# Fused memory attention and two-layer MLP on one core: order of the start, halves of the first weights, and the place of every operation from a table

## The chip, the cores and the metric

The kernel runs on one NeuronCore of a Trainium2 chip. The metric is device microseconds of one execution: three runs of the kernel before took 557.5, 558.44 and 559.41 us, median 558.44. The profiled execution has a span (first to last instruction) of 555.3 us. Engines are named as in the profile: PE (TensorE products), PEld (its weight loads), DVE (VectorE), ACT (ScalarE), POOL (GpSimd) and SP, whose queue issues every DMA here.

## The reference

For 4 batches, 8 heads, 576 rows and head size 64, causal softmax attention is mixed by a gate with a linear memory read, and the result, as 2304 rows of 512, goes through a two-layer MLP with a leaky unit. Inputs are 64-bit or 32-bit floats as given; the MLP's weights arrive as 64-bit floats.

```python
scores = scale * np.matmul(q, k.transpose(0, 1, 3, 2))      # causal mask, softmax -> a
local = np.matmul(a, v)
q_p = np.where(q > 0, q, np.exp(q) - 1.0) + 1.0
mem_out = (q_p @ M_prev) / (q_p . z_prev + 1e-6)
x = g * mem_out + (1 - g) * local                           # g = sigmoid(beta), per head
h = x.reshape(2304, 512) @ w_in                             # 512 x 2048
out = (np.maximum(h, 0) + alpha * np.minimum(h, 0)) @ w_out # 2048 x 512
```

## The kernel before, in words

Rows are worked in nine groups of 256. Group Z (called the first group here) holds the first 64 rows of each of the four batches; each batch's other 512 rows make two groups, of row blocks 1 and 2 and of row blocks 3 and 4. The first group is short attention in f32 (64 keys), and so are blocks 1 and 2 of batch 0; all later groups split each f32 operand into two f16 parts and multiply three of the four combinations.

A group's way is this. Scores (PE, tile s) go through mask and row minimum on DVE, exponent with row sum on ACT, and a scaling into two f16 parts P on ACT and DVE (`unit_probs`; the memory read's columns come from POOL). SP transposes P by a DMA into PT. PE multiplies PT with the values into tile bank (`pair_values`, for two heads at a time, a "pair" here), ACT and DVE make the two f16 parts xn, SP transposes them into x. Then `moe_in` gives tile h (PE), ACT and DVE make the leaky unit's r and gg, and `moe_out` gives tile y (PE), which ACT scales to the output. A step j of the MLP is 256 of the 2048 hidden columns; h has two PSUM buffers and y two.

The weights arrive as raw 64-bit words in pieces of two times 512 KB, `load_w`. For each, `conv_w` builds f32 on DVE with three bit operations (`to_f32`, lines 770 to 777) over 1024 columns, and ACT adds up their squares; from the sums come power-of-two scales. The first half of w_in and w_out (pieces 0 to 3 and 4 to 7) is used in f32 by the first group and by batch 0's first group (steps 0 to 3), and all pieces are then split into f16 parts. Where the first group begins, `load_first` fetches its q, z, k, v and M rows, `first_scores` and `first_values` make its attention, and `WARM` gives 16 + 50 products of a constant (tile h from ones) that nothing reads; they keep PE working while the first transfers land.

The order of all this is not the order in the file. `Work.add` records each operation with its dependencies and an estimated price (`price`), and `issue` (line 532) lays out all engines by list scheduling with ranks that a table of biases by phase (`STAGES`) shifts, over three passes (`lay`, line 462). What comes out is one order of all operations; each engine then runs its own in that order, and so does SP's queue with the DMAs. Nearly every operation is issued from line 560, so the profile is read by tiles. Names: q_0_93 (q2_0) holds the first group's q rows, R the big weight buffer in which also the first group's k, v and M rows stand, kn and E staging for weights, k_65 and v_66 the turned keys and the split values.

Of the kernel before, what the change touches and what calls it, by code (L numbers as in the profile page):

```python
# [2 lines left out]

# [21 lines left out]
WARM = 16, 50  # L25
# [6 lines left out]
STAGES = [  # L32
    (2, {
        "A0": 10.6, "A:DVE": 50.6, "BK0": 102.5, "BK:ACT": -27.7, "BK:PE": 3.4, "C0": -56.4, "C1": 22.3, "C2": 335.8,
        "C3": -920, "C:ACT": 1096.2, "C:DVE": -3.8, "C:PE": -943.6, "I": -699.2, "I:DVE": 79.2, "I:POOL": 497.7,
        "J:ACT": 470.6, "J:DVE": 108, "J:PE": -179.3, "K": 47.5, "K:POOL": 2.3, "L0K": -713.8, "L0K:DMA": 228.2,
# [6 lines left out]
        "LW:DMA": 605.3, "LZ": 27.3, "LZ:DMA": -1145.9, "Lz": 8.5, "Lz:DMA": -8.6, "N": 87.9, "N:PE": 292.5,  # L43
        "P01": 4, "P03": 3.7, "P11": 777.2, "P13": 823.4, "P21": 168.1, "P23": 236.6, "P31": -675.3, "P33": -247.2,
        "P:ACT": 988.7, "P:DMA": 668.5, "P:DVE": -882.6, "P:PE": -157.8, "S0": 4737.2, "S1": -1253, "S3": -2953.6,
        "S:ACT": -87.5, "S:DVE": 168.1, "V0": -874.8, "V:DVE": 211.2, "V:PE": -90.8, "a0": 5.7, "a1": 46.8,
        "a2": -161.5, "a3": 389.6, "a4": -42.9, "a:ACT": -265.2, "a:DVE": 239.4, "bk0": -173.5, "bk1": 344.8,
        "bk2": 244.5, "bk3": 3.1, "bk:ACT": -687.5, "bk:DMA": 246.9, "bk:DVE": 1380.7, "bk:PE": 100.3, "bv0": -0.7,
# [5 lines left out]
        "o31": 144.8, "o33": 10.1, "o:ACT": -779.8, "o:DMA": 580.1, "o:DVE": -613.6, "o:PE": 33.3, "oZ": 10.8,  # L54
# [14 lines left out]
        "C3:PE": -8.9, "C:ACT": 13.2, "C:DVE": 9.3, "C:PE": -17.2, "I": -57.9, "I:POOL": -8.6, "J:ACT": -18.7,  # L69
# [6 lines left out]
        "LW3": -8.7, "LW3:DMA": -22.1, "LW:DMA": -2.8, "LZ:DMA": -42.6, "Lz:DMA": -4.4, "N": 0.9, "N:PE": -13.7,  # L76
# [5 lines left out]
        "P33:DMA": -3.8, "P33:DVE": -7.4, "P33:POOL": -37, "P:ACT": 15, "P:DMA": -20.1, "P:DVE": 8.9, "P:PE": -86.4,  # L82
# [481 lines left out]
def kernel(  # L564
# [27 lines left out]
    Z = B  # L592
# [1008 lines left out]
```

## Time and profile before

| | kernel before |
|---|---|
| runs, us | 557.5, 558.44, 559.41 (median 558.44) |
| span of the profiled execution, us | 555.3 |
| PE busy | 532.3 us (96%), 4421 products |
| PEld busy | 353.1 us (64%) |
| DVE busy | 451.2 us (81%), 1197 instructions |
| ACT busy | 376.1 us (68%) |
| POOL busy | 77.7 us (14%) |
| mean granted PE clock | 0.985 |
| HBM | 35.66 MB read, 5.77 MB written |

The median of the runs is 3.1 us above the profiled execution's span; that distance is taken to hold for the changed kernel too. The page gives busy shares, and in 40 equal slices of 13.9 us the busy tenths of each engine and the granted PE clock in tenths of 2.4 GHz (a 5 is 1.2 GHz). A PE record ends when the product has left the array, so records of products that follow each other overlap, and what PE can do in a stretch is read from the distance of their starts. The stage views give busy time in chosen stretches.

### The profile page before, as it was taken

The page shows a single profiled execution, that of the slowest core. Times are in us where ns is not written, and L with a number is a line of the kernel's source. Part 1 is how long each engine was busy: PE and PEld are TensorE (multiplying, and loading weights), DVE is VectorE, ACT ScalarE, POOL GpSimd, SP SyncE. Part 2 cuts the span into 40 slices and gives each one's busy share as a digit, 9 for nine tenths or more (in the row PEclk, how much of TensorE's full clock was granted, in tenths as well). Part 3 has the DMA queues.
Part 4 walks back from the last instruction along what each step waited for, and adds up shares of the span by engine and source line. Part 5 has one row for each costly group of instructions (what it writes and reads, how often), then busy time and mean ns, then how long its engine had stood idle before and what let it go on. Part 6 is the DMA issues. An engine that isn't in the chain of part 4 may idle for free.

```text
span 555.3 us, 11994 instructions
## 1 busy us (share of the span) xinstructions
PE 532.3 (96%) x4421; PEld 353.1 (64%) x4421; DVE 451.2 (81%) x1197; ACT 376.1 (68%) x790; POOL 77.7 (14%) x142
## 2 busy tenths in 40 slices
PE   9739999999999899999998999999999999999997
PEld 3438655666567566758566667667677676866573
DVE  4899999999999899999998899997678885333322
ACT  2558987768999378978867887786587874222312
POOL 2000510031030011311221200321021120000000
PEclk9869999999999999999999999999999999999999
DMA  8999685827359999379998737599536665000101
GB/s 288 231 339 204 192 238 176 246 74 170 91 115 183 219 228 199 86 154 205 221 188 190 170 79 170 130 200 190 79 81 121 138 138 133 21 2 1 38 1 38
DMA packets 226026, 82.84 MB, mean 149 GB/s; under 512 B 216224, under 2 KB 216240, under 8 KB 225968
## 3 DMA queue, kind: packets, MB, share of 16 engines
q1 hardware_dynamic: 225968, 82.09, 64.0%
q8 instruction: 34, 0.56, 0.4%
q14 instruction: 24, 0.20, 0.1%
HBM read 35.66 MB, written 5.77 MB: 75 GB/s over the span
## 4 chain that ended last, share of the span: by engine, by line
PE 52%; DVE 30%; DMA 5%; issue 5%; ACT 3%; SPq 2%; POOL 2%; DVEq 0%; POOLq 0%; ACTq 0%
PE y L560 22%; PE h L560 20%; DVE R L560 5%; DVE P L560 5%; PE s L560 5%; DVE E L560 4%; PE bank L560 4%; DVE gg L560 3%; DVE r L560 3%; DVE q L560 2%; SPq L560 2%; POOL E L560 2%; DMA xn<-in_moe_alpha_dram 1%; DMA k<-k 1%; DVE t L560 1%
## 5 line engine op out<-in xcount | busy, mean ns | idle before, releaser
L560 PE MATMUL h<-x,R 128*128 128x256 f16 x1536 | 261.8, 273 | 1.7 <-DMA x<-xn 1.7
L560 PE MATMUL y<-R,gg 128*128 128x512 f16 (+1 forms) x832 | 258.3, 397 | 0.4 <-ACT k L560 0.4
L560 PE MATMUL bank<-v,PT 128*128 128x64 f16 x1224 | 179.2, 193 | 2.7 <-DMA PT<-P 2.3
L560 PEld LDWEIGHTS <-R 128*128 128x128 f16 x1536 | 148.9, 98 | 41.9 <-issue 5.6
L560 PEld LDWEIGHTS <-PT 128*128 128x128 f16 x1224 | 113.9, 98 | 10.5 <-DMA PT<-P 4.1
L560 PEld LDWEIGHTS <-gg 128*128 128x128 f16 x768 | 74.6, 98 | 70.8 <-DVE gg L560 0.5
L560 POOL TENSOR_SCALAR E<-q,nrm,sm 128x64 f32<-128x64 f32 x112 | 62.5, 570 | 316.8 <-DVE sm L560 265.1
L560 ACT ACTIVATE E<-E,mx 128x320 f32<-128x320 f32 (+3 forms) x136 | 81.0, 601 | 22.7 <-DVE mx L560 18.3
L560 DVE SCALAR_TENSOR_TENSOR P<-E,mx,P 128x384 f16<-128x384 f32 (+2 forms) x112 | 75.4, 699 | 9.8 <-ACT P L560 9.7
L560 ACT ACTIVATE P<-E,mx 128x384 f16<-128x384 f32 (+2 forms) x112 | 70.4, 673 | 16.4 <-POOL E L560 13.2
L560 DVE SCALAR_TENSOR_TENSOR r<-r,oma,h 128x256 f32<-128x256 f32 x128 | 56.8, 473 | 25.0 <-ACT r L560 24.7
L560 DVE SCALAR_TENSOR_TENSOR gg<-r,gsc,gg 128x512 f16<-128x512 f32 x56 | 41.7, 746 | 32.4 <-ACT gg L560 20.6
L560 ACT ACTIVATE r<-h 128x512 f32<-128x512 f32 x72 | 42.0, 586 | 37.2 <-PE h L560 23.1
L560 ACT ACTIVATE gg<-r,gsc 128x512 f16<-128x512 f32 x56 | 39.9, 715 | 32.2 <-PE y L560 29.0
L560 DVE CUSTOM_DVE_ANT_0 E<-s,mask,pm 128x320 f32<-128x320 f32 (+2 forms) x96 | 56.8, 609 | 1.4 <-PE s L560 1.2
L560 PE MATMUL s<-k,qT 128*128 128x64 f16 (+5 forms) x136 | 37.4, 294 | 1.2 <-DMA k<-k 1.0
L560 PE MATMUL s<-k,qS 128*128 128x192 f16 (+4 forms) x120 | 33.6, 294 | 0.0
L560 PE MATMUL h<-R 128*128 128x256 f32 x128 | 32.9, 384 | 0.0
L560 PEld LDWEIGHTS h<-R 128*128 128x128 f32 x128 | 22.3, 192 | 6.6 <-issue 3.3
L560 ACT ACTIVATION_READ_ACCUMULATOR E<-E,mx 128x1 f32 x124 | 23.4, 188 | 0.0
L560 ACT ACTIVATE R<-R,wsc 128x1024 f16<-128x1024 f32 x16 | 18.3, 1142 | 4.0 <-DVE R L560 4.0
L560 DVE SCALAR_TENSOR_TENSOR R<-R,wsc 128x1024 f16<-128x1024 f32 x16 | 20.4, 1275 | 0.4 <-ACT R L560 0.4
(183 smaller groups left out, 619.6 us busy)
## 6 DMA issues: line engine op xcount, KB each, us to landing
q<-in_q_dram SPq DMA_DIRECT2D x16, 256.0 KB, 4.3
vn<-in_v_dram SPq DMA_DIRECT2D x16, 256.0 KB, 4.9
out_dram<-t SPq DMA_DIRECT2D x16, 256.0 KB, 2.7
kn<-in_moe_w_in_dram SPq DMA_DIRECT2D x6, 512.0 KB, 6.5
kn<-in_moe_w_out_dram SPq DMA_DIRECT2D x6, 512.0 KB, 5.7
kn<-in_k_dram SPq DMA_DIRECT2D x12, 256.0 KB, 3.9
qS<-qT SPq DMA_DIRECT2D x24, 128.0 KB, 3.0
R<-in_moe_w_in_dram SPq DMA_DIRECT2D x4, 512.0 KB, 5.6
```

The source lines that it names most:

```text
L560: fn(*a, **kw)
```

## The change

The planner goes: `lay`, the biases and the passes are taken out, and a table `PLACES` gives, for each phase, the place of each of its operations in the one order of all. Phases get finer names (one per head, pair, step or piece), so that the table can place them singly. Beside that, six things differ in what is executed.

1. Warming products: 16 + 24 instead of 16 + 50.
2. Pieces 0 to 3 of the weights (the half of w_in that is used first) are loaded and converted in two column halves of 512 KB and 512 columns; all four first halves are recorded ahead of the second ones, so that the first steps of `moe_in` need the first halves alone.
3. After each first half, two f32 products of 256 columns into the warming tile (`PACE`), eight in all, which nothing reads.
4. The first group's v and M rows come in two transfers of 256 KB each instead of four of 128 KB.
5. The squares of pieces 0 to 3 are written to R[0] and not over the staging.
6. In the first group the turned q and P use tile y and no longer tile h.

```diff
-WARM = 16, 50
+WARM = 16, 24
+PACE = 2
+PLACES = {
+    "LK0": (
+        "79 84"
+    ),
...
     def issue(self, tc):
...
-        for passes, bias in STAGES:
...
+        places = {k: iter(map(int, x.split())) for k, x in PLACES.items()}
+        at = [next(places[op[7]]) for op in self.ops]
         with tc.manual_schedule():
-            for i in sorted(range(len(ops)), key=lambda i: (start[i], i)):
-                _, fn, a, kw = ops[i][:4]
+            for i in sorted(range(len(at)), key=at.__getitem__):
+                _, fn, a, kw = self.ops[i][:4]
                 fn(*a, **kw)
...
-        for b in range(B):
-            vv = nat[Z]["v"][b // 2][:, b % 2]
-            Y.dma_start(out=vv[64:128], in_=v[b, :, 0:64, :].rearrange("h p d -> p h d"))
-            Y.dma_start(out=vv[0:64], in_=M_prev[b].rearrange("h d e -> d h e"))
+        for t in range(2):
+            work.phase = f"LV{t}"
+            for ps, src in ((slice(64, 128), v[2 * t:2 * t + 2, :, 0:64, :]), (slice(0, 64), M_prev[2 * t:2 * t + 2])):
+                Y.dma_start(out=nat[Z]["v"][t][ps].rearrange("p b h d -> p (b h) d"), in_=src.rearrange("b h p d -> p (b h) d"))
...
-    def load_w(s):
+    def load_w(s, cs=(0, 1)):
...
-        for c in range(2):
+        for c in cs:
...
+        if s < 4 and not cs[0]:
+            work.phase = f"n{s}"
+            for i in range(PACE):
+                T.matmul(h0[:, 0], lhsT=r[:, 0:128], rhs=r[:, 0:256], start=True, stop=True)
+            work.phase = f"C0{s}"
+        if cs[-1]:
+            pieces.pop(s)
+            work.phase = f"c{s // 4}"
+            A.activation(R[0] if s < 4 else st[:, 0:1024], r, AF.Square, scale=2.0 ** -20, accum_out=wsq[s // 4][:, s % 4:s % 4 + 1])
...
     def weights(i):
-        load_w(8 * i)
-        for s in range(8 * i, 8 * i + 8):
+        if i == 0:
+            for f in (load_w, conv_w):
+                for c in range(2):
+                    for s in range(4):
+                        f(s, (c,))
+            w_scale(0)
+        first = 8 * i if i else 4
```

How the order moves is seen at three places. The first is SP's queue at the start of the program. Before, it begins:

```order
L560 DMA R<-in_moe_w_in_dram 128x1024 x4
L560 DMA kn_90<-in_moe_w_in_dram 128x1024
L560 DMA xn_103<-in_moe_alpha_dram 16x128
L560 DMA q_1_94<-in_z_prev_dram 64x512 x4
L560 DMA kn_90<-in_moe_w_in_dram 128x1024
L560 DMA gco<-in_beta_dram 128x8
L560 DMA E_0_92<-in_moe_w_in_dram 128x1024 x2
L560 DMA q_0_93<-in_q_dram 64x8x64
L560 DMA R<-in_k_dram 64x8x64
L560 DMA q_0_93<-in_q_dram 64x8x64 x3
```

and in the changed kernel the same queue begins:

```order
L1742 DMA R<-in_moe_w_in_dram 128x1024
L1742 DMA R<-in_v_dram 64x16x64
L1742 DMA R<-in_M_prev_dram 64x16x64
L1742 DMA gco<-in_beta_dram 128x8
L1742 DMA q_0_93<-in_q_dram 64x8x64
L1742 DMA xn_103<-in_moe_alpha_dram 16x128
L1742 DMA q_0_93<-in_q_dram 64x8x64
L1742 DMA R<-in_M_prev_dram 64x16x64
L1742 DMA R<-in_v_dram 64x16x64
L1742 DMA q_0_93<-in_q_dram 64x8x64 x2
L1742 DMA R<-in_k_dram 64x8x64
```

One half piece of w_in leads, then the first group's rows; the other seven half pieces stand behind the last k rows. Before, all eight stand ahead of the first q row.

The second place is DVE's queue, with the first group's softmax (ISA is the masked row minimum, P the first group's probabilities). Before, its normalization is followed by the conversion of w_out, as w_in's is long done:

```order
L560 TENSOR_TENSOR P_100<-q_0_93,nrm_105 128x8x64
L560 RECIPROCAL zsm_135<-zsm_135 128x8
L560 RECIPROCAL zsm_136<-zsm_136 128x8
L560 TENSOR_TENSOR P_99<-P_99,zsm_135 128x8x64
L560 TENSOR_TENSOR P_100<-P_100,zsm_136 128x8x64
L560 TENSOR_REDUCE wsc<-bank_67 128x1
```

and in the changed kernel the conversion of w_in in halves stands there, among the minima of the second half of the rows (zmx_134):

```order
L1742 TENSOR_TENSOR P_99<-P_99,zsm_135 128x8x64
L1742 TENSOR_SCALAR R<-R 128x512
L1742 ISA P_100,zmx_134<-s_0_68,mz 128x64
L1742 ISA zmx_134 128x1
L1742 SCALAR_TENSOR_TENSOR R<-R 128x512
L1742 TENSOR_SCALAR R<-E_0_92 128x512
```

Seven of the eight half conversions have moved behind the minima of the first half of the rows (zmx_133); before, all of w_in stood ahead of them.

The third place is PE where the values of the thirteenth pair begin (heads 0 and 1 of batch 2, blocks 1 and 2; bank is their tile). Before, 584 f16 products of h and 299 products of y stand ahead of the first of them:

```order
L560 LDWEIGHTS gg_150
L560 MATMUL y_132<-R,gg_150 128x512
L560 LDWEIGHTS R
L560 MATMUL h_123<-x_110,R 128x256
L560 LDWEIGHTS gg_150
L560 MATMUL y_131<-R,gg_150 128x512
L560 LDWEIGHTS PT_115
L560 MATMUL bank_67<-v_66,PT_115 128x64
```

and in the changed kernel 621 and 320:

```order
L1742 LDWEIGHTS R
L1742 MATMUL h_124<-x_111,R 128x256
L1742 LDWEIGHTS PT_115
L1742 MATMUL bank_67<-v_66,PT_115 128x64
L1742 LDWEIGHTS PT_115
L1742 MATMUL bank_67<-v_66,PT_115 128x64
L1742 LDWEIGHTS qT
L1742 MATMUL s_0_69<-k_65,qT 128x320
```

More of the MLP has moved ahead of this pair, and its products stand closer together.

## Rows read from the trace of the kernel before

**Rows 1.** The page: busy times, and granted PE clock in 40 slices.
```profile
PE 532.3 (96%) x4421; PEld 353.1 (64%) x4421; DVE 451.2 (81%) x1197; ACT 376.1 (68%) x790; POOL 77.7 (14%) x142
PEclk9869999999999999999999999999999999999999
```
**Rows 2.** Stretches: length, busy PE, PEld, DVE, ACT, POOL, PEclk, DMA share, GB/s.
```profile
0.00:47.30 47.30, 34.45 (x243) 20.93 (x243) 37.42 (x110) 23.70 (x65) 4.16 (x13) 0.82 0.97 275
47.30:555.30 508.00, 497.88 (x4179) 332.19 (x4178) 413.82 (x1088) 352.40 (x726) 73.53 (x129) 1.00 0.62 137
...
0.00:6.00 6.00, 4.96 (x12) 1.81 (x13) 0.23 (x3) 1.03 (x1) 4.16 (x13) 1.00 0.66 216
6.00:12.00 6.00, 5.73 (x27) 2.50 (x26) 5.46 (x8) 1.41 (x3) 0.00 (x0) 1.00 1.01 337
...
18.00:24.00 6.00, 3.09 (x21) 1.78 (x19) 5.97 (x12) 5.22 (x10) 0.00 (x0) 0.92 0.91 193
24.00:30.00 6.00, 5.28 (x68) 4.30 (x66) 4.84 (x33) 4.57 (x18) 0.00 (x0) 0.51 0.97 215
...
400.00:540.00 140.00, 140.00 (x1266) 96.72 (x1264) 76.28 (x189) 69.20 (x140) 11.51 (x26) 1.00 0.30 69
```
**Rows 3.** PE in order of time, 18 to 50 us: start, length, work.
```profile
18.91 0.66 PE L560 MATMUL h<-ident,q 128*128 128x128 f32 x4
...
23.76 0.48 PE L560 MATMUL s<-q,k 128*64 128x64 f32 x4 [2.43 <-ACT q L560]
...
43.78 2.27 PE L560 MATMUL s<-PT,R 128*64 128x64 f32 x60
...
47.34 2.86 PE L560 MATMUL h<-R 128*128 128x256 f32 x12
```
**Rows 4.** SP's queue in order of time; DMA issues: KB each, us to landing.
```profile
11.78 0.66 SPq L560 DMA_DIRECT2D q<-in_q_dram  x1
...
18.48 1.31 SPq L560 DMA_DIRECT2D R<-in_k_dram  x2
...
R<-in_k_dram SPq DMA_DIRECT2D x4, 128.0 KB, 3.5
```
**Rows 5.** DVE in order of time, 6 to 51 us.
```profile
6.24 0.69 DVE L560 TENSOR_SCALAR R<-R 128x1024 int32<-128x1024 int32 x1 [5.12 <-DMA R<-in_moe_w_in_dram]
...
27.72 0.23 DVE L560 CUSTOM_DVE_ANT_0 P<-s,mz 128x64 f32<-128x64 f32 x1 [1.11 <-PE s L560]
...
45.07 1.22 DVE L560 SCALAR_TENSOR_TENSOR R<-R 128x1024 int32<-128x1024 int32 x1
...
50.21 0.69 DVE L560 SCALAR_TENSOR_TENSOR q<-q,t 128x512 f32<-128x512 f32 x1
```
**Rows 6.** ACT in order of time, 28 to 47 us.
```profile
28.34 0.34 ACT L560 ACTIVATE P<-P,zmx 128x64 f32<-128x64 f32 x1
...
45.97 1.31 ACT L560 ACTIVATE R<-s,xsc 128x512 f32<-128x512 f32 x2 [0.24 <-PE s L560]
```
**Rows 7.** The thirteenth pair in order of time: DVE, SP, PE.
```profile
293.60 0.48 DVE L560 SCALAR_TENSOR_TENSOR P<-E,mx,P 128x256 f16<-128x256 f32 x1
...
293.52 4.80 SPq L560 DMA_TRANSPOSE PT<-P  x2
...
298.92 0.20 PE L560 MATMUL bank<-v,PT 128*128 128x64 f16 x1 [1.75 <-DMA PT<-P]
```
**Rows 8.** Costliest PE groups by form: busy us, mean ns, idle before.
```profile
L560 PE MATMUL h<-x,R 128*128 128x256 f16 x1536 | 261.8, 273 | 1.7 <-DMA x<-xn 1.7
L560 PE MATMUL y<-R,gg 128*128 128x512 f16 x768 | 225.4, 380 | 0.0
L560 PE MATMUL bank<-v,PT 128*128 128x64 f16 x1224 | 179.2, 193 | 2.7 <-DMA PT<-P 2.3 <-DVE xn L560 0.4
```
**Rows 9.** PE in order of time, unbroken runs of one kind.
```profile
507.27 3.69 PE L560 MATMUL h<-x,R 128*128 128x256 f16 x32
...
521.63 3.19 PE L560 MATMUL y<-R,gg 128*128 128x512 f16 x14
```

More of the change, by code (lines that the diff above doesn't have):

```diff
@@ L1 @@
 from contextlib import ExitStack
-from heapq import heappop, heappush
 import concourse.bass as bass
@@ L392, in add @@
             hold, move, late, packets = hold
+            late += LATE
         elif kind == "PE":
@@ L460, in lag @@
         return self.LAGS[self.ops[d][0]].get(self.ops[i][0], 0)
-    def lay(self, before, after, rank, back=False):
-        ops = self.ops
-        left = [len(x) for x in before]
-        at, start = [0.0] * len(ops), [0.0] * len(ops)
-        kinds = ("PE", "DVE", "ACT", "POOL", "DMA")
-        free = dict.fromkeys(kinds, 0.0)
-        wait = {x: [] for x in kinds}
-        ready = {x: [] for x in kinds}
-        wire = 0.0
-        ring, told = [(0.0, 0.0, 0.0)], 0
-        turn, used, warm, mode = WINDOW, 0.0, False, 0
-        for i, op in enumerate(ops):
-            if not left[i]:
-                heappush(wait[op[0]], (0.0, i))
-        todo = len(ops)
-        while todo:
-            best = None
-            for x in kinds:
-                while wait[x] and wait[x][0][0] <= free[x]:
-                    i = heappop(wait[x])[1]
-                    heappush(ready[x], (rank[i], i))
-                t = free[x] if ready[x] else wait[x][0][0] if wait[x] else None
-                if t is not None and (best is None or t < best[0]):
-                    best = t, x
-            t, x = best
-            if not ready[x]:
-                free[x] = t
-                continue
-            i = heappop(ready[x])[1]
-            start[i] = t
-            todo -= 1
-            hold, (move, late, both, packets) = ops[i][5], ops[i][8]
-            if x == "DMA" and not back:
-                begun = max(wire, t + 100)
-                wire = begun + move
-                free[x] = max(t + hold, wire - 350) if packets < 0 else t + hold
-                ring.append((begun, wire, ring[-1][2] + max(packets, 0)))
-                gone = ring[-1][2] - RING
-                if gone > 0:
-                    while ring[told][2] < gone:
-                        told += 1
-                    b, e, c = ring[told]
-                    was = ring[told - 1][2] if told else 0.0
-                    free[x] = max(free[x], b + (e - b) * (gone - was) / (c - was) if c > was else e)
-                done = wire + late
-            else:
-                if x == "DMA":
-                    hold = max(hold, move)
-                elif x == "PE" and not back:
-                    while t >= turn:
-                        warm = used >= (0.08 if warm else 0.8) * WINDOW
-                        turn, used = turn + WINDOW, 0.0
-                    if packets != mode:
-                        hold += (95 if packets else 0) + (0, 0, 150, 200)[mode]
-                    mode = packets
-                    if not warm:
-                        hold *= 2
-                    used += hold * late
-                elif both and not back and free["POOL"] > t:
-                    hold += SHARE * (free["POOL"] - t)
-                free[x] = done = t + hold
-            for f, lag in after[i]:
-                at[f] = max(at[f], done + lag + (ops[f][8][1] if back and ops[f][0] == "DMA" else 0))
-                left[f] -= 1
-                if not left[f]:
-                    heappush(wait[ops[f][0]], (at[f], f))
-        return start
@@ L532, in issue @@
-    def issue(self, tc):
-        ops = self.ops
-        before = [[(d, self.lag(d, i)) for d in op[4]] for i, op in enumerate(ops)]
-        after = [[] for _ in ops]
-        for i, ds in enumerate(before):
-            for d, lag in ds:
-                after[d].append((i, lag))
-        late = [0.0] * len(ops)
-        hold = [max(op[5], op[8][0]) for op in ops]
-        pe = 0.0
-        for i in reversed(range(len(ops))):
-            took = ops[i][8][0] + ops[i][8][1] if ops[i][0] == "DMA" else hold[i]
-            late[i] = min([late[f] - lag for f, lag in after[i]], default=0.0) - took
-            if ops[i][6]:
-                late[i] = pe = min(late[i], pe - hold[i])
-        rank = late
-        for passes, bias in STAGES:
-            rank = [x + 1e3 * sum(bias.get(k, 0) for k in dict.fromkeys((
-                op[7], op[7].rstrip("0123456789_") + ":" + op[0], op[7] + ":" + op[0]))) for x, op in zip(rank, ops)]
-            for n in range(passes):
-                if n:
-                    back = self.lay(after, before, [-s - h for s, h in zip(start, hold)], True)
-                    rank = [-s - h for s, h in zip(back, hold)]
-                start = self.lay(before, after, rank)
-            rank = start
@@ L805, in load_w, with conv_w @@
             Y.dma_start(out=st[:, 1024 * c:1024 * c + 1024].bitcast(I32), in_=src)
-    def conv_w(s):
-        work.phase = f"C{s // 4}"
-        r, st = raw(s + 1), pieces.pop(s)
-        n = 1024 if WC[s] else 512
-        for c in range(0, 1024, n):
-            to_f32(r[:, c:c + n], st[:, 2 * c:2 * c + 2 * n].bitcast(I32).rearrange("p (c t) -> p c t", t=2))
-        A.activation(st[:, 0:1024], r, AF.Square, scale=2.0 ** -20, accum_out=wsq[s // 4][:, s % 4:s % 4 + 1])
+    def conv_w(s, cs=(0, 1)):
+        work.phase = f"C{s // 4}{s % 4}" if s > 3 or not cs[0] else f"D0{s}"
+        r, st = raw(s + 1), pieces[s]
+        for c in (0, 512) if len(cs) == 1 or not WC[s] else (0,):
+            n = 512 if len(cs) == 1 or not WC[s] else 1024
+            if len(cs) == 1 and c != 512 * cs[0]:
+                continue
+            to_f32(r[:, c:c + n], st[:, 2 * c:2 * c + 2 * n].bitcast(I32).rearrange("p (c t) -> p c t", t=2))
+        if s < 4 and not cs[0]:
[7 more added lines that the diff above has]
+            A.activation(R[0] if s < 4 else st[:, 0:1024], r, AF.Square, scale=2.0 ** -20, accum_out=wsq[s // 4][:, s % 4:s % 4 + 1])
     def w_scale(i):
+        work.phase = f"c{i}"
         pt = o_sc[:, 136:140]
@@ L825, in w_kappa @@
     def w_kappa(hf):
+        work.phase = f"c{2 * hf + 1}"
         i = 2 * hf + 1
@@ L989, in prep_phi @@
         nrm, tt, C = p["nrm"][:, r], p["tt"][:, r], p["C"][:, :, r]
+        ph = work.phase
         for i in range(i0, i1):
+            work.phase = f"{ph}{i}"
             qi = qs[i]
@@ L1024, in build_qk @@
     def build_qk(b, hp):
-        work.phase = f"bk{b}"
+        work.phase = f"bk{b}{hp}"
         n, p = nat[b], pre[b]
@@ L1042, in build_v @@
     def build_v(b, hp):
-        work.phase = f"bv{b}"
+        work.phase = f"bv{b}{hp}"
         n, p = nat[b], pre[b]
@@ L1074, in first_pair @@
     def first_pair(hp, bl):
-        work.phase = f"s0{bl[0]}"
+        work.phase = f"s0{bl[0]}{2 * hp + 1}"
         p = pre[0]
@@ L1107, in unit_scores @@
             return
-        work.phase = f"s{b}{bl[0]}"
+        work.phase = f"s{b}{bl[0]}{h}"
         a = h % 2
@@ L1129, in unit_probs @@
     def unit_probs(b, h, bl):
-        work.phase = f"P{b}{bl[0]}"
+        work.phase = f"P{b}{bl[0]}{h}"
         p = pre[b]
@@ L1257, in first_values @@
     def first_values(t, x32):
-        work.phase = "oZ"
+        work.phase = f"oZ{t}"
         n, p = nat[Z], pre[Z]
@@ L1283, in moe_in @@
     def moe_in(g, j):
-        work.phase = f"h{g['id']}{j // 4}"
+        work.phase = f"h{g['id']}{j // 4}{j % 4}"
         n = g["n"]
@@ L1323, in moe_out @@
     def moe_out(g, j):
-        work.phase = f"y{g['id']}{j // 4}"
+        work.phase = f"y{g['id']}{j // 4}{j % 4}"
         n = g["n"]
@@ L1470, in weights @@
     def weights(i):
-        load_w(8 * i)
-        for s in range(8 * i, 8 * i + 8):
+        if i == 0:
[5 more added lines that the diff above has]
+        first = 8 * i if i else 4
+        load_w(first)
+        for s in range(first, 8 * i + 8):
             if s % 8 < 7:
```

1539 lines of the change are left out of this document (1481 added, 58 removed), and 276 rows, old and new, of the table STAGES.

## The prediction

> **What bounds the kernel now.** I read the page's busy times and clock first. PE is busy for 96% of the span, and its clock is low only in slices 2 and 3 of 40 [rows 1]. So I went to the stretches. Up to 47.3 us PE is busy for 34.5 us at a mean clock of 0.82, and some 14 us of that are the 66 warming products (512 columns, 0.216 us as worked out below); from 47.3 to the end it is busy for 497.9 of 508.0 us [rows 2]. The first product of the MLP starts at 47.34 [rows 3]. The reader is to see two kernels: a start, in which PE waits for the first group's attention, and 508 us in which it hardly waits. The order of time tells what the start waits for. q's rows are issued at 11.78, the last k rows at 18.5 [rows 4], as the whole first half of w_in goes before them. Turning q begins at 18.91, the first scores stand at 23.76, the first minimum on DVE at 27.72, the values at 43.78 [rows 3, 5].
>
> After 47.3 two engines are full. DVE is busy for 413.8 of the 508.0 us, but little of its idle time lies early: from 400 to 540 it works 76.3 of 140 us [rows 2]. So DVE sets the pace up to some 400 us, and PE that of the end. Where PE waits in the middle, it waits for DVE's work: at the thirteenth pair DVE ends the last P at 294.1, the DMA turns it, and PE, idle for 1.75 us, begins the values at 298.9 [rows 7].
>
> **The start.** What leads now is one half piece of w_in (0.5 MB) and the first group's rows, 2.6 MB by 0.52 MB each for q, k, z, v and M. Weights moved at 337 GB/s between 6 and 12 us, the rows at 193 to 215 between 18 and 30 [rows 2]. In the first 6 us 216 GB/s came to 1.3 MB, at 337 GB/s 3.85 us of moving, so moving begins near 2.2 us. Then 1.6 us for the half piece and 2.6 MB at 204 GB/s, 12.8 us: the last k lands near 16.6, with the rest of its way (3.5 us from issue to landing for 128 KB [rows 4], of which 0.6 us is moving) near 17.5, against about 22 before. The first half piece lands 1.6 us sooner than the two pieces did that DVE waited for at 6.24 [rows 5], so at 4.7.
>
> DVE's work before the first minimum is 11 us, estimated from its queue at the lengths of [rows 5]: one half conversion 1.6, two reductions of 1024 columns at 1.2, eight instructions of 512 at 0.65, some twenty small ones at 0.1. So it reaches the minimum at 16 to 17.5, when the first half's scores are there. From there eight exponents at 0.33 us [rows 6] with two copies, eight more, the normalization on DVE (from the first minimum 9 us of DVE's queue to the second half's P, estimated in the same way: sixteen minima at 0.15, four products of 512 at 0.65, six conversion steps and small ones), turning, the values (2.3 us [rows 3]) and the scaling (0.65 us each [rows 6]) bring the first group's x near 31. The first column halves of the four pieces are converted by 30: 11.5 us of DVE's queue after the first minimum, and their transfers, four of 0.52 MB at 337 GB/s behind the last k, land by 24. So PE's first MLP product starts near 31 and not at 47.3: 16 us.
>
> **Why not 16 us.** That is PE's gain. DVE's queue isn't shortened by it. DVE was idle for 47.3 - 37.4 = 9.9 us up to there [rows 2]. Of that remain 4.4 us before the first half piece (4.7 less the 0.3 of the memsets) and about 2 us for the scores: 6.5, or 3.4 us less. The halves cost something: a half of 512 columns takes 0.69 us and a whole 1.22 [rows 5]; twice 0.69 less 1.22 is 0.16 us for each of 12 instructions, 1.9 us at most, and 0.5 if the records overlap as these two kinds' starts do. I take 0.5, since DVE is full there.
>
> So DVE gives 3 us and PE 16. What the end gains depends on how the table places PE's work against DVE's. Where DVE paces, count what stands ahead of the same point in both orders. Up to the values of the thirteenth pair, PE has 37 more products of h and 21 more of y behind it. Unbroken, h starts every 3.42/31 = 0.110 us, y every 2.81/13 = 0.216 [rows 9]: 4.1 + 4.5 = 8.6 us, less 0.5 for four score products that now come later: 8.1 us of useful work done sooner. DVE, up to the last P of this pair, has by the same count 3.8 us more in front (0.5 the halves, 1.6 values' low parts, 2.1 the leaky unit, 0.4 one xn, less 0.8 reductions and minima that come later). So this pair begins 3.8 - 3.4 = 0.4 us later than before, with 8.1 us less left for PE behind it: 7.7 us. At the seventeenth pair the same count gives DVE +1.0 us, h -3 and y +13 (2.5 us): -2.4 and -2.5, 4.9 us. I take the thirteenth, as it is the pair with a wait of PE; at the seventeenth PE did not idle.
>
> **The rest of the change.** 26 warming products fewer are 26 x 0.216 = 5.6 us of PE, in time when PE waited anyway: nothing, as long as the first transfers are what PE waits for. The eight pacing products (f32, 256 columns, two records each, 2.86/12 = 0.24 us a record [rows 3]) are 3.8 us; four stand in the wait for the first group, four among the first steps, 1.9 us, where PE is ahead of DVE, so nothing; without that cover 1.9. Without warm clock the first group's products cost double: between 24 and 30 us the clock was 0.51 [rows 2] in the same kind of work, so this is as before. Four v and M transfers less save SP 4 x 0.65 us, behind which k's rows stand; that is in the 17.5. Squares to R[0] and tile y for h take buffers away from waits; bounds 0 and -1, I take 0.
>
> A product of the same loop costs the same: the table removes none beside the warming ones. Sum: 555.3 - 7.7 = 547.6 us of span, and 3.1 us around it (558.4 - 555.3) give 550.7.
>
> The trace says that PE is 98% busy after 47.3 us, but a record of h lasts 273 ns [rows 8] and the next starts after 110 [rows 9], so busy is no measure of full. The Trainium skill's page Trainium Kernel Development and Optimization, section Performance Expectations, says the same more sharply: matmul busy time is a bad metric for the distance to the roof, the weight loads' busy share a good one. Here PEld is busy for 332 of 508 us, 65% [rows 2]. By that rule a better packing could take more than the start gives; that is the second rival.
>
> **Rivals.**
> 1. PE keeps its whole start. For it: DVE has 63.7 us to spare between 400 and 540 [rows 2], so a table could have put off DVE's work enough. Against it: the counts above, 3.8 us more of DVE's work before the thirteenth pair. Price: 16 less the 1.9 of pacing, 14.1: 541.2 + 3.1 = 544.
> 2. The dense part gets denser. h and y in f16 alone are 1536 x 0.110 + 768 x 0.216 = 335 of the 508 us; values are 193 - 163 = 30 ns each beside them (163 being what h's 273 exceed its 110): 37 us. If the new order packed away the 10.1 us in which PE is idle after 47.3, beside the 7.7: 537.5 + 3.1 = 541. Against it: that idle time is in many small waits, and 3.8 us of it at the end.
> 3. The gain is given back. DVE's idle time stays 9.9 and the seventeenth pair decides: 4.9 - 3.4 = 1.5 us: 557. For it: its early part is already full.
> 4. Slower: the rows land late. DVE works in order, and behind the first minimum stand seven half conversions that no longer fill the wait. If the rows move at 120 GB/s and not 204, because nothing but pieces of 256 bytes (64 f32) is then in the queues, k lands 9 us later, DVE idles for 15.5 us and the thirteenth pair is 9.4 us later; with 8.1 us of PE's work done sooner the end comes 1.3 us later, 559.7; at 100 GB/s, 13 us later, 564. It is slower once DVE is idle for more than about 14 us before its second half conversion. Against it: the same transfers moved at 193 or more with weights among them.
>
> **Numbers.** Forecast (gain of 2 to 11 us) 0.52: 547.5 to 556.5. Rivals 1 and 2 together 0.20: 540 to 547.5. Rival 3: 0.12, 556.7 to 560. Rival 4: 0.16, beyond 560. A measurement of this kernel tells about 0.3%, 1.7 us, from no change. Faster by more than that: 0.52 + 0.20 = 0.72; within 0.12; slower 0.16. The range leaves out slower than 560 for the most part, and gains over 18 us: 540 to 560. The likeliest case's own range is 547.5 to 556.5.
>
> **What would show it.** Right: PE's first run of f32 products of h near 31 us; first scores near 15 and first minimum near 17; DVE idle for 6 to 7 us before 40; the thirteenth pair's values near 299 with some 8 us less of h and y behind them; PE without waits after 400. Wrong: k landing after 22; DVE idle before its minima for more than 10 us; waits of PE for P or PT between 100 and 350 us that add up to more than 16 us (then even the 7.7 is not kept) or to less than 5 (then rival 1); a clock of 0.5 after 47 us.

## The result: 1.2% faster, as far as forecast, with two terms off

Four executions of the changed kernel took 550.29 to 553.72 us, median 551.71, against 558.28 before; the ratio is 0.9883, 95% interval [0.985, 0.9916], 6.6 us less. The forecast was 550.7 us in a range of 540 to 560. Each of the four lies 1.8 us above its span; the profiled one took 553.72 us, the longest of them, with a span of 551.9.

The page of the changed kernel, busy times and granted clock in 40 slices, answers to [rows 1]:

```profile
PE 528.5 (96%) x4411; PEld 355.0 (64%) x4411; DVE 452.7 (82%) x1209; ACT 376.5 (68%) x790; POOL 67.9 (12%) x142
...
PEclk9879999999997999999999999999999999999999
```

PE is busy for 3.8 us less, DVE for 1.5 us more, and PE's clock now also drops in slice 13. The stretches answer to [rows 2] (length, busy PE, PEld, DVE, ACT, POOL, clock, DMA share, GB/s):

```profile
0.00:47.30 47.30, 39.27 (x278) 27.58 (x279) 36.11 (x122) 25.71 (x68) 4.27 (x13) 0.89 1.01 243
47.30:551.90 504.60, 489.23 (x4134) 327.46 (x4133) 416.62 (x1088) 350.78 (x722) 63.66 (x129) 0.99 0.63 141
0.00:6.00 6.00, 4.95 (x12) 1.80 (x13) 0.23 (x3) 1.28 (x1) 4.27 (x13) 1.00 0.72 137
6.00:12.00 6.00, 4.21 (x20) 1.74 (x19) 3.82 (x11) 1.47 (x3) 0.00 (x0) 1.00 1.05 167
18.00:24.00 6.00, 3.67 (x48) 2.90 (x50) 5.91 (x35) 3.73 (x11) 0.00 (x0) 1.00 1.04 277
24.00:30.00 6.00, 3.38 (x46) 2.84 (x48) 6.00 (x31) 5.50 (x30) 0.00 (x0) 0.72 1.10 330
400.00:540.00 140.00, 139.20 (x1237) 96.42 (x1236) 78.81 (x197) 71.75 (x148) 13.71 (x28) 1.00 0.33 71
```

The transfers of the first 12 us came at 137 and 167 GB/s, where before it was 216 and 337. DVE is idle for 47.3 - 36.11 = 11.2 us up to 47.3, not for 6.5. PE's order of time answers to [rows 3]:

```profile
13.41 1.12 PE L1742 MATMUL y<-ident,q 128*128 128x128 f32 x4
...
20.24 1.15 PE L1742 MATMUL s<-q,k 128*64 128x64 f32 x32 [1.26 <-ACT q L1742]
...
29.64 2.03 PE L1742 MATMUL s<-PT,R 128*64 128x64 f32 x32 [0.46 <-ACT PT L1742]
...
36.49 7.96 PE L1742 MATMUL h<-R 128*128 128x256 f32 x36
```

Scores, values and the run of f32 products of h all come sooner than before, at 20.24, 29.64 and 36.49 us (forecast: 15, and 31 for the last). SP's queue shows one cause ([rows 4]; start, length):

```profile
2.69 3.34 SPq L1742 DMA_DIRECT2D gco<-in_beta_dram  x1
6.07 0.60 SPq L1742 DMA_DIRECT2D q<-in_q_dram  x1
...
15.16 1.30 SPq L1742 DMA_DIRECT2D R<-in_k_dram  x2
```

Behind the first half piece and two transfers of rows, SP is held for 3.34 us at beta's small transfer, so q's rows start at 6.07 and the last k rows at 15.16. DVE ([rows 5]) starts no sooner than before. Behind the first half piece the rows are queued at once, and the two share the DMA engines; with other half pieces behind it, in the run with the weights first below, DVE's wait for it is 1.7 us shorter:

```profile
6.56 0.43 DVE L1742 TENSOR_SCALAR R<-R 128x512 int32<-128x512 int32 x1 [5.45 <-DMA R<-in_moe_w_in_dram]
...
21.63 0.21 DVE L1742 CUSTOM_DVE_ANT_0 P<-s,mz 128x64 f32<-128x64 f32 x1
...
46.42 0.87 DVE L1742 SCALAR_TENSOR_TENSOR gg<-r,oma,h 128x256 f32<-128x256 f32 x2 [0.82 <-ACT r L1742]
```

The thirteenth pair ([rows 7]) has its last P in the row that follows, and its first product of values begins at 303.74, against 298.92 before:

```profile
298.69 0.48 DVE L1742 SCALAR_TENSOR_TENSOR P<-E,mx,P 128x256 f16<-128x256 f32 x1
```

Now the ledger by which the forecast was made. For each kernel two stretches are read: from the start to the end of that P, and from the pair's first product of values to the end of the span. The kernel before:

```profile
0.00:294.08 294.08, 277.38 (x2130) 179.00 (x2131) 277.20 (x747) 221.95 (x477) 47.48 (x82) 0.97 0.81 193
298.92:555.30 256.38, 251.85 (x2264) 171.90 (x2264) 170.76 (x441) 151.89 (x308) 28.13 (x56) 1.00 0.45 98
```

The changed kernel:

```profile
0.00:299.17 299.17, 280.60 (x2162) 183.96 (x2163) 281.61 (x764) 226.62 (x479) 36.98 (x82) 0.97 0.82 191
303.74:551.90 248.16, 243.36 (x2212) 167.33 (x2209) 167.18 (x432) 146.27 (x301) 29.44 (x56) 1.00 0.47 99
```

Up to that P, DVE works 281.61 and not 277.20 us, and is idle for 17.56 (299.17 - 281.61) and not 16.88. From the values on, 248.16 us are left and not 256.38: 8.2 us less, as forecast (8.1). But the pair comes 4.8 us later, not 0.4.

### The profile page after: what moved, and what is told of

Its sections match the earlier page's. It is cut to its first block, busy times and chain, and to the rows that moved or that the text cites. A ratio compares the mean times of both kernels' runs of the same rounds, so it can differ in the third digit from the quotient of the medians.

```text
span 551.9 us, 11931 instructions
## 1 busy us (share of the span) xinstructions
PE 528.5 (96%) x4411; PEld 355.0 (64%) x4411; DVE 452.7 (82%) x1209; ACT 376.5 (68%) x790; POOL 67.9 (12%) x142
## 4 chain that ended last, share of the span: by engine, by line
PE 45%; DVE 11%; DMA 4%; ACT 2%; issue 2%; POOL 1%; ACTq 0%; DVEq 0%; SPq 0%
PE h L1742 19%; PE y L1742 19%; PE bank L1742 3%; PE s L1742 3%; DVE P L1742 2%; DVE E L1742 2%; DMA x<-xn 2%; DVE r L1742 1%; DMA qT<-q 1%; DVE gg L1742 1%; DMA PT<-P 1%; DVE q L1742 1%; ACT E L1742 1%; ACT P L1742 1%; DVE k L1742 1%
## 5 line engine op out<-in xcount | busy, mean ns | idle before, releaser
L1742 PE MATMUL y<-R,gg 128*128 128x512 f16 (+1 forms) x832 | 237.5, 400 | 1.4 <-ACT t L1742 0.8
L1742 PE MATMUL h<-x,R 128*128 128x256 f16 x1536 | 216.7, 273 | 3.5 <-DVE r L1742 1.9
L1742 PEld LDWEIGHTS <-R 128*128 128x128 f16 x1536 | 145.0, 98 | 47.0 <-issue 6.9
L1742 POOL TENSOR_SCALAR E<-q,nrm,sm 128x64 f32<-128x64 f32 x112 | 55.5, 508 | 334.1 <-DVE sm L1742 223.5
L1742 DVE SCALAR_TENSOR_TENSOR P<-E,mx,P 128x640 f16<-128x640 f32 (+3 forms) x112 | 76.2, 699 | 11.7 <-ACT P L1742 11.5
L1742 ACT ACTIVATE P<-E,mx 128x512 f16<-128x512 f32 (+3 forms) x112 | 72.3, 673 | 16.0 <-POOL E L1742 8.1
L1742 PE MATMUL bank<-v,PT 128*128 128x64 f16 x1224 | 81.2, 193 | 0.9 <-DMA PT<-P 0.6
L1742 PEld LDWEIGHTS <-PT 128*128 128x128 f16 x1224 | 64.7, 98 | 18.1 <-issue 1.2
L1742 DVE CUSTOM_DVE_ANT_0 E<-s,mask,pm 128x320 f32<-128x320 f32 (+3 forms) x96 | 57.8, 612 | 3.7 <-PE s L1742 2.5
L1742 PE MATMUL s<-k,qT 128*128 128x512 f16 (+5 forms) x136 | 37.1, 289 | 2.3 <-DVE mx L1742 2.3
```

The costliest lines, as they stand in the source:

```text
L1742: fn(*a, **kw)
```

## Experiments

In all runs the kernel before ran beside them; ratios are to it, with the 95% interval, and as the runs were taken on several chips, kernels are compared by these ratios. "Pair" is the end of the thirteenth pair's last P in the profiled execution, "idle" DVE's idle time up to there, "rest" the time from the pair's values to the end, all read as in the ledger.

| kernel | ratio | pair | DVE busy | idle | rest |
|---|---|---|---|---|---|
| before | 1 | 294.08 | 277.20 | 16.88 | 256.38 |
| before, second trace | | 297.40 | 277.71 | 19.69 | 255.87 |
| changed | 0.9883 [0.985, 0.9916] | 299.17 | 281.61 | 17.56 | 248.16 |
| changed, again | 0.9889 [0.9867, 0.9911] | 297.57 | 281.48 | 16.09 | 248.28 |
| PE 4.3 us more | 0.9929 [0.9907, 0.9951] | 297.69 | 281.23 | 16.46 | 247.41 |
| DVE 4.2 us more | 1.0132 [1.0107, 1.0156] | 310.85 | 287.01 | 23.84 | 249.64 |
| weights first | 1.0062 [1.0038, 1.0086] | 307.30 | 283.18 | 24.12 | 248.04 |
| beta first | 0.9869 [0.9846, 0.9892] | 295.43 | 281.03 | 14.40 | 247.76 |
| 26 warming products back | 0.989 [0.9868, 0.9912] | 298.40 | 281.28 | 17.12 | 247.35 |
| no pacing | 0.9829 [0.9807, 0.9852] | 293.98 | 280.77 | 13.21 | 247.72 |
| z on POOL | 0.9948 [0.993, 0.9965] | 297.34 | 280.29 | 17.05 | 249.64 |
| z left out | 0.982 [0.9789, 0.9851] | 294.74 | 277.10 | 17.64 | 247.62 |
| beta first, no pacing | 0.9797 [0.9771, 0.9824] | 293.45 | 281.05 | 12.40 | 247.46 |
| the same, PE's waits filled | 0.9845 [0.9813, 0.9876] | 295.94 | 281.34 | 14.60 | 248.18 |

The last column is the first result. Whatever was done ahead of the pair, 247 to 250 us were left behind it; only the kernel before has 256. So the end is set by when this pair comes. That DVE's busy and idle time add up to the pair's time is bookkeeping, which would hold for any engine; which engine the pair waits for has to be asked by delaying engines.

**The two kernels once more.**

> The changed kernel once more, beside the others. All theories: 550 to 554 us, ratio near 0.988. Its profile is a second sample of where PE waits: in the first profile PE waits 1.51 us and 1.88 us for DVE at 171 and 174 us and its clock is 0.5 from 175 to 180 us. If that is the order's doing, the same two waits stand here; if it is this one execution's, they are gone and the span is near 548.5 us.

The second trace of the changed kernel has a span of 550.4 us, and the pair 1.6 us sooner. PE's waits at 171 and 174 us and the clock of 0.5 behind them stand there again (0.91 over 170 to 210 us), so they belong to the order.

> The kernel before once more, for a second trace. The changed kernel's runs lie 1.8 us above their spans. If that holds for the kernel before, the first trace's execution (span 555.3 us) took 557.1 us, a short one, and this one's span is 555 to 557 us with the last P of the thirteenth pair at 293.9 to 296 us.

It took 559.5 us with a span of 557.7: 1.8 us around the span here as well; span and pair (297.40) lie past what was expected. By this distance the first trace was of a short execution, 557.1 us. With two traces of each, the pair comes 2.6 us later ((299.17 + 297.57 - 294.08 - 297.40) / 2): DVE's work 4.1 us more, its idle time 1.5 us less. With 7.9 us less left that makes 5.3 us of the 6.6 measured; single traces differ by 3 us.

**Delay PE or DVE alone.** Near 80 us, in front of a step of h:

```diff
...
+    work.phase = "XP"
+    for i in range(20):
+        T.matmul(h0, lhsT=ones[:, 0:64].bitcast(F16), rhs=ones.bitcast(F16)[:, None, :].to_broadcast([128, 2, 256]),
+                 start=True, stop=True)
```

> Twenty more products of the constant (512 columns, 0.216 us each, 4.3 us of PE) in front of a step of h that PE reaches near 80 us; nothing reads them. Theory D (DVE sets the pace up to the thirteenth pair): PE's waits behind that point (10.5 us between 47 and 304 us in the first profile) take the delay up, the thirteenth pair's values stay near 303.6 and the end moves by less than 1.5 us. Theory P (PE sets the pace in the middle as well): the end moves by 3.5 to 4.3 us, to 555 or 556 us.

```diff
...
+    junk = cp.tile([128, 4], F32, name="junk")
...
+    work.phase = "XD"
+    for i in range(7):
+        V.reduce_max(junk, ones[:, None, :].to_broadcast([128, 4, 128]), axis=AX.X)
```

> Seven more reductions of 512 columns on DVE (0.60 us from start to start, 4.2 us) at the same place, near 80 us; nothing reads them. Theory D: the last P of the thirteenth pair 4 us later, near 303, the end 3 to 4.2 us later, near 555 us. Theory P: DVE's idle time (6.2 us between 47 and 299 us) and its 60 us to spare after 400 us take it up, the end moves by less than 1.5 us.

PE's 4.3 us are taken up in the trace (pair at 297.69 instead of 297.57), but that trace is of the shortest of six executions (551.22). The median is 2.2 us later (553.93 against 551.73), half of the delay and between the theories, with intervals that meet. So it isn't shown that PE's work in the middle is free. DVE's 4.2 us cost 12.4 (564.15): theory P falls, and theory D is too mild. DVE's work grew by 5.5 us and its waits by 7.7. The row of that kernel from 47.3 to 130 us, and those of SP's queue (start, length):

```profile
47.30:130.00 82.70, 77.28 (x327) 44.66 (x326) 80.15 (x207) 58.77 (x132) 8.78 (x20) 0.94 0.71 178
```

```profile
266.16 6.44 SPq L1745 DMA_TRANSPOSE PT<-P  x2
272.65 3.86 SPq L1745 DMA_DIRECT2D kn<-in_k_dram  x5
276.61 4.05 SPq L1745 DMA_TRANSPOSE qT<-q  x1
```

The turning of P for two heads holds SP for 6.44 us, the loads of k for the next batch 3.86, the turning of q 4.05. In the changed kernel the same three rows, some 7 us earlier, are 5.90, 3.62 and 2.05 us (second trace):

```profile
259.00 5.90 SPq L1742 DMA_TRANSPOSE PT<-P  x2
264.95 3.62 SPq L1742 DMA_DIRECT2D kn<-in_k_dram  x5
268.67 2.05 SPq L1742 DMA_TRANSPOSE qT<-q  x1
```

PE then waits 1.8 and 3.0 us for PT at 285 and 297 us. A delay of DVE shifts its transposes against the loads of the next batch, and both take longer. This bears on the second part of the loss only. Against the second trace of the changed kernel, the first of DVE's f16 P is 6.0 us later (116.63 against 110.64), 1.8 us more than was put in: behind the seven reductions PE is busy for 1.8 of 5 us (80 to 85 us), its clock is then 0.50 and 0.55 up to 95 us, and DVE waits for scores. The distance stays at 6.0 to 6.4 us up to 238 us and grows to 13.3 at the pair. That the transposes and loads are all of these 6.9 us isn't shown.

**Less work for DVE.** The product of q with z, for batches 1 to 3:

```diff
-PZ = [1, 1, 1, 1, 1]
+PZ = [1, 0, 0, 0, 1]
```

> The products of q with z of batches 1 to 3 (twelve of 512 columns, 0.60 us of DVE each from start to start) go to POOL at the same places. Theory D: 4.8 us less of DVE's work ahead of the thirteenth pair, less what DVE waits for POOL in front of the reductions; the thirteenth pair 2 to 4 us sooner and the end with it, 548 to 550 us. Theory P, or DVE's waits taking all of it: 551 to 554 us.

Slower by 0.6% instead. Eight of the twelve products stand ahead of the pair, 5.4 us by 0.68 each, but DVE's busy time fell by 1.2 us only: its other instructions took 4.2 us more. The POOL group of that kernel (busy us, mean ns), and DVE's scaling of k there:

```profile
L1742 POOL TENSOR_TENSOR t<-q,zb 128x512 f32<-128x512 f32 x12 | 17.6, 1471 | 33.4 <-DVE q L1742 23.8 <-ACT E L1742 3.7 <-ACT k L1742 3.0
```

```profile
L1742 DVE SCALAR_TENSOR_TENSOR k<-kn,scr,k 128x640 f16<-128x640 f32 x12 | 11.5, 957 | 0.0
```

and that scaling in the changed kernel:

```profile
L1742 DVE SCALAR_TENSOR_TENSOR k<-kn,scr,k 128x640 f16<-128x640 f32 x12 | 10.5, 874 | 0.0
```

On POOL a product takes 1.47 us, and the same instruction of DVE goes from 874 to 957 ns. The Trainium skill's page Perfetto Trace Analysis, section Optimizing Scalar/DVE Operations, says that the two engines share a read port of SBUF, so that moving work between them may not help; the trace agrees.

```diff
...
-            (V if PZ[b] else G).tensor_tensor(e, qi, n["z"][i], op=ALU.mult)
+            if b in (0, Z):
+                V.tensor_tensor(e, qi, n["z"][i], op=ALU.mult)
```

> Leaves out the products of q with z of batches 1 to 3 (twelve on DVE, 0.60 us each), so that the reductions read q's exponent instead; all else as in the changed kernel. On POOL they saved nothing (554.6 us), and in that trace DVE's other instructions took 7 us more. Theory D: without them 4.8 us of DVE's work ahead of the thirteenth pair are gone, the pair comes 4 to 5 us sooner, the end 4 to 5 us sooner, 547 us. If DVE's work in the middle were not what the pair waits for: 550 to 552 us.

548.81 us, 0.7% less than the changed kernel. DVE's work fell by 4.4 us, but its waits grew by 1.5 and the pair came 2.8 us sooner. Of these 2.8 us, 1.8 stand already at 128 us, where no product is changed yet (the first that is changed stands near 160 us): in this execution PE's clock was 1.00 and not 0.72 from 24 to 36 us. In the trace with z on POOL it was 0.86, with the same 1.8 us. The last P of the first f16 pairs in the second trace of the changed kernel, and here:

```profile
128.42 1.54 DVE L1742 SCALAR_TENSOR_TENSOR P<-E,mx,P 128x512 f16<-128x512 f32 x2
```

```profile
126.59 1.54 DVE L1742 SCALAR_TENSOR_TENSOR P<-E,mx,P 128x512 f16<-128x512 f32 x2
```

So the trace gives 4.4 us less of DVE's work only 1.0 us at the pair, and z on POOL made the pair 1.6 us later. DVE is part of what the pair waits for, not all: what it gains it mostly spends waiting for others. How much of the 0.7% is the edit's, and how much a better clock at the start, isn't shown.

**What leads the queue.** The eight half pieces and their conversions in front, as before the change (places 6, 7, 33 and 34 in the table):

```diff
     "LW01": (
-        "121"
+        "6"
...
     "C01": (
-        "235 260 262"
+        "33 33 33"
```

> The changed kernel with the eight half pieces of w_in issued ahead of the first group's rows, and their conversions ahead of DVE's first reduction, as before; all else stays where the table has it. Theory D (what counts is DVE's work and idle time up to the thirteenth pair): DVE converts while the rows come, its idle time up to 47.3 us falls from 11.2 to 8 or 9 us, and though PE's run of f32 h products begins near 41 and not at 36.5 us the end moves by less than 2 us to either side. Rival (the gain is the earlier start of PE): 4 to 6 us later, 555 to 558 us.

Both expectations are passed: 9.1 us later (560.85), with 8 us more of DVE's idle time up to the pair (24.12); my expectation of less had the wrong sign. DVE's waits up to 131 us (us in total, times, longest):

```profile
DVE q L1742 <- ACT t L1742: 10.0, 2, 7.5
DVE R L1742 <- DMA R<-in_moe_w_in_dram: 3.7, 1, 3.7
```

The wait for the first half piece is 1.7 us shorter than in the changed kernel (3.7 against 5.45), but behind the first group's minima DVE now waits 10.0 us for ACT, 7.5 of it at once (1.2 in all in the changed kernel): PE and ACT are at the first group's values, and the seven half conversions that filled this time are done. PE's run of f32 products of h begins later as well, at 45.86 and not at 36.11:

```profile
45.86 7.95 PE L1742 MATMUL h<-R 128*128 128x256 f32 x36
```

That is 9.8 us, about as much as the end. So the order of the start is worth 9 us in this table, whose other places were made for the other order, and that is more than all that the change gains. But DVE's waits and PE's later start come together here, and this run doesn't tell which of them the end follows.

```diff
     "Lz": (
-        "21 15"
+        "21 7"
```

> Beta's transfer goes directly behind the first half piece, ahead of the first v and M rows; in the changed kernel it stands behind them and holds SP for 3.34 us at 2.69. Theory A (SP's queue is held by the many small pieces of the rows before it): the hold moves to the next transfer, the rows land as before, 550 to 553 us. Theory B (beta's own transfer is slow): the hold goes, the first minimum comes near 19 and not at 21.6 us, DVE's idle time up to 47.3 us falls from 11.2 to some 8.5 us, and by theory D the end comes 2 to 3 us sooner, 549 us.

550.13 us. SP's hold moves to the next transfer, q's, and is half as long:

```profile
1.20 0.42 SPq L1742 DMA_DIRECT2D gco<-in_beta_dram  x1
...
3.17 1.83 SPq L1742 DMA_DIRECT2D q<-in_q_dram  x1
```

So by these rows it is the queue behind the rows for a part, and beta for another. DVE waits 1.7 us less up to the pair. The gain, 0.2%, is within the intervals.

**The warming and the pacing products.**

```diff
-WARM = 16, 24
+WARM = 16, 50
...
```

> The 26 warming products are back (16 + 50), spread over the places of the 24. The prediction costs them at nothing, as PE waits there: 550 to 553 us. Theory D with the trace: 42 of them now stand ahead of alpha's turning (29 take 8.9 us from 1.05 us), which then begins near 14 and not at 10 us; DVE waits there, its idle time up to 47.3 us grows by 2 to 3 us, and the end comes 2 to 3 us later, 554 us.

551.78 us, no change, as the prediction has it; theory D's 2 to 3 us are seen only as 1 us more of DVE's idle time. PE's run of f32 products of h begins 2.5 us later than in the second trace of the changed kernel, and the end does not follow:

```profile
38.62 7.96 PE L1742 MATMUL h<-R 128*128 128x256 f32 x36
```

```diff
-PACE = 2
+PACE = 0
```

> Without the eight pacing products. The prediction costs them at nothing: 550 to 553 us. If they hold the clock up: the granted clock up to 47.3 us falls below 0.89, the first group's products take longer, DVE waits, 1 to 2 us later. If they stand in the way of the first group's products: up to 1.9 us sooner.

548.08 us, 0.6% sooner: 3.3 us by the ratios. The pair comes at 293.98, where it came before the change:

```profile
0.00:293.98 293.98, 275.06 (x2145) 180.18 (x2146) 280.77 (x764) 226.61 (x479) 37.42 (x82) 0.98 0.84 194
298.99:546.70 247.71, 243.06 (x2212) 167.33 (x2209) 167.07 (x432) 146.28 (x301) 29.51 (x56) 1.00 0.47 99
```

DVE is idle for 13.21 us up to there, 3.7 less than in the first trace before (16.88). The forecast had 3.4 less, a pair 0.4 later and a span of 547.6; this kernel's span is 546.7. So the eight products stood in the way. In the changed kernel two of them stand in a wait of PE, one each at 31.01 and 33.52 between the first group's own products, and four in PE's first run of h (two records each; the second trace, then the kernel without them):

```profile
29.05 2.03 PE L1742 MATMUL s<-PT,R 128*64 128x64 f32 x32 [0.46 <-ACT PT L1742]
31.01 1.22 PE L1742 MATMUL h<-R 128*128 128x256 f32 x2
...
33.52 0.60 PE L1742 MATMUL h<-R 128*128 128x256 f32 x2
34.05 1.20 PE L1742 MATMUL s<-PT,R 128*64 128x64 f32 x32
...
36.11 7.95 PE L1742 MATMUL h<-R 128*128 128x256 f32 x36
```

```profile
32.49 2.03 PE L1742 MATMUL s<-PT,R 128*64 128x64 f32 x32
...
35.58 6.21 PE L1742 MATMUL h<-R 128*128 128x256 f32 x28
```

At 31.01 and 33.52 PE spends 1.22 and 0.60 us on them, and the second values begin at 34.05; without them at 32.49, though the clock is lower then (0.57 against 0.72 from 24 to 36 us). The run of h has 36 records with them and 28 without, and ends at 44.06 and at 41.79. Of the 3.6 us by which the pair comes sooner than in the second trace, 0.5 stand at the first product gg of DVE near 41 us. 0.9 more stand at the next, as DVE no longer waits there for ACT's r (0.79 us; the same wait is shown above at 46.42, in the first trace), and 0.8 at 93 us, where a wait for a transfer of w_in is gone. Where the other 1.3 arise isn't shown.

> Beta's transfer behind the first half piece, and no pacing products: 1.6 and 3.6 us sooner each by itself. If both take DVE's idle time of the start away at different places, they add: 546 to 547 us. If they take the same idle time: 548 us.

548.19 us, ratio 0.9797, 0.9% below the changed kernel: by the ratios the two edits add (0.2% and 0.6%), and this is the lowest ratio here, though its interval overlaps that of the kernel without pacing.

**PE's start once more.** That kernel, with PE's waits filled by products of the constant, seven in front of the second scores and nine in front of the turning of P:

```diff
...
+    for i in range(16):
+        work.phase = "XV" if i < 7 else "XW"
+        T.matmul(h0, lhsT=ones[:, 0:64].bitcast(F16), rhs=ones.bitcast(F16)[:, None, :].to_broadcast([128, 2, 256]),
+                 start=True, stop=True)
```

> Beta's transfer first, no pacing products, and sixteen products of the constant (0.216 us each) in two waits of PE that stand in the trace without pacing: seven ahead of the first group's second scores (1.85 us of waiting), nine ahead of the turning of its P (2.19 us). Without them the granted clock is 0.5 from 24 to 34 us. If these waits are what lets the clock fall: it stays near 1.0, the turnings and values of 25.4 to 34.8 us take 6 and not 9.3 us, PE's run of f32 h products begins 1.5 to 3 us sooner, and by theory D the end comes 0.5 to 1 us sooner, as far as DVE's last waits of the start (1.3 us) go: 546.5 to 547.5 us. If the products only stand in the way: 548 to 549 us. If the clock of the start is worth its 3 us to the end: 545 us.

The clock does what was hoped. The stretch without the products, and with them:

```profile
24.00:36.00 12.00, 10.10 (x94) 9.00 (x95) 11.60 (x36) 7.76 (x26) 0.00 (x0) 0.58 1.04 267
```

```profile
24.00:36.00 12.00, 10.60 (x115) 8.25 (x112) 11.98 (x42) 9.83 (x33) 0.00 (x0) 1.00 1.01 253
```

It is 1.00 and not 0.58 from 24 to 36 us, and over the whole span it is 0.991 to 0.994 in all six executions, against 0.983 to 0.990 without the products. The run of f32 products of h begins at 33.03 and not at 34.79:

```profile
34.79 6.21 PE L1742 MATMUL h<-R 128*128 128x256 f32 x28
```

```profile
33.03 6.23 PE L1748 MATMUL h<-R 128*128 128x256 f32 x28
```

And yet the kernel is no faster, 550.94 us: 0.5% slower by the ratios, whose intervals overlap by 0.1%. DVE now waits for w_out's transfers:

```profile
42.31 0.69 DVE L1748 TENSOR_SCALAR R<-R 128x1024 int32<-128x1024 int32 x1 [0.99 <-DMA R<-in_moe_w_out_dram]
...
46.55 0.69 DVE L1748 TENSOR_SCALAR R<-R 128x1024 int32<-128x1024 int32 x1 [0.23 <-DMA R<-in_moe_w_out_dram]
...
50.15 0.69 DVE L1748 TENSOR_SCALAR R<-E 128x1024 int32<-128x1024 int32 x1 [0.52 <-DMA E<-in_moe_w_out_dram]
...
54.89 0.69 DVE L1748 TENSOR_SCALAR R<-kn 128x1024 int32<-128x1024 int32 x1 [0.52 <-DMA kn<-in_moe_w_out_dram]
```

These are 0.99 + 0.23 + 0.52 + 0.52 = 2.3 us, of which one of 0.2 us stands in the kernel without them. What PE and DVE win in the first group they lose at the next transfer; the DMA engines' share is 1.02 up to 47.3 us in that kernel, so they seem to have no time to spare there.

## Why the prediction was right, and where it was not

- **What is left behind the pair.** Right, and the main step: 8.1 us less were forecast, 7.9 measured over two traces each, 8.2 in the first. From 400 to 540 us PE is idle for 0.8 us.
- **Which engine the pair waits for.** DVE for the most part, as forecast: its delay comes through whole and more, that of PE by half. No run puts the 37 and 21 products back behind the pair, so that their place alone makes the 8 us is counted, not tested.
- **DVE's extra work ahead of the pair.** Forecast 3.8 us, measured 4.1.
- **DVE's idle time, the mis-sized term.** Forecast 3.4 us less, measured 1.5 less over two traces each. And these 1.5 are not where the forecast put them: up to 47.3 us DVE is idle for 1.1 us longer than before (11.2 and 10.9 us against 9.9 and 10.0), and from there to the pair for 2.6 us less (5.8 against 8.4 on average), where the sum counted nothing. The row rate was taken as 204 GB/s and measured 137 to 201 up to 18 us; the first half piece came at 6.56 and not at 4.7, as rows were queued right behind it; and SP was held for 3.34 us.
- **"The eight pacing products are 3.8 us ... so nothing."** This failed. They cost 3.3 us, nearly their length, and without them the pair comes when the forecast had it. Two and not four stand in a wait, two stand between steps of the first group, and the four in the first run of h have no cover: DVE waits behind that run. The bound of 1.9 was too low.
- **The 26 warming products.** Nothing, right: 551.78 against 551.73.
- **16 us for PE's start.** Mis-sized, 10.9 (47.34 - 36.49), but the sum did not use it. A start 2.5 us later (the warming products back) or 1.8 sooner (the waits filled) doesn't bring the end with it; with the weights first it is 9.8 later and the end 9, with DVE's waits beside it. The early start is not idle all the same: from 47.3 us to the pair's last P, PE was idle for 3.9 us before (6.3 in the second trace), so the 8.6 us of products that now stand ahead of the pair would not have fitted there.
- **Around the span.** 3.1 us were put down to it, from a median beside a shorter execution; it is 1.7 to 2.0 us in all executions but one (2.5). The span was forecast as 547.6 us and is 549.9 in the median of the four executions, 2.3 more; that the time is only 1.0 us above the forecast is luck, by this error of 1.3.
- **Rivals.** The first (PE keeps its start) did not come: 10.9 of 16 us were there, and the pair came later, not sooner. The second: from 47.3 on PE's waits grew from 10.1 to 15.4 us and the weight loads' share stays 65% (327.46 / 504.6), so nothing got denser. The third came by half: DVE's idle time of the start did not fall (11.2 us and not 6.5), but the time left behind the thirteenth pair fell by all that was forecast. The fourth did not come: DVE was idle for 9.2 us before its first minimum at 21.63, not for 14; but the run with the weights first shows that its kind of price is there, 9 us where the half conversions do not fill DVE's wait for the first group.
- **Signs.** Two signs of being wrong appeared, and the gain came all the same. A clock of 0.5 came behind 47 us (175 to 180 us), and PE's waits for P and PT from 100 to 350 us are below 5 us (0.6 for PT), though rival 1 did not come. The second was no sign, as the kernel before has it too (2.3 for PT).

## What to carry to other kernels

Find the point behind which the remaining time no longer changes, and count the pacing engine's work and waits ahead of it; that sum holds for any engine, so delay each engine to see which one paces. A product that only keeps the clock up has to be placed by the waits of the changed order: twenty-six among the first waits cost nothing, but eight, of which six stood among the steps of the chain, cost 3.3 us. And a higher clock in itself gained nothing here, as the next wait took it. Compare one trace with another only after a second trace of each: here single executions of one kernel differ by 1.6 and 3.3 us at the point that decides.

## What the runs showed of the hardware

- Four executions of what is the same program up to 160 us were granted 0.72, 0.72, 0.86 and 1.00 of PE's clock from 24 to 36 us (the changed kernel twice, and the two with z moved or left out). With 0.72 the last P of the first of the f16 pairs ended at 130.1 and 130.0 us, with 0.86 and 1.00 at 128.1. Executions of the changed kernel spread over 550.3 to 553.7 us; without the pacing products four lay within 0.7 us.
- SP's queue stood behind transfers of rows in pieces of 256 bytes: for 2.9 to 3.5 us at beta's 4 KB in the eight traces in which it follows the first half piece and the first v and M rows, and for 2.9 to 4.8 us at a piece of w_in behind q's rows in the eleven traces of the changed order. The size of the pieces was not varied.
- PE's two waits near 171 and 174 us were followed by a clock of 0.50 from 175 to 180 us, while PE was busy for 4.7 of 5 us. With DVE's seven reductions PE was busy for 1.8 of 5 us from 80 to 85 us, and the clock was 0.50 and 0.55 in the next two stretches of 5 us.
